# Side matrix products between attention steps: from pairs of groups that end together to a staggered chain, with one product of each step moved forward

## The chip, the cores and the metric

The kernel runs on one core of one Trainium2 chip. The metric is the device time of one execution in microseconds; the kernel before takes 1770.66 us in the median of three runs (1768.67 to 1771.16). TensorE does matrix products into PSUM (8 banks of 128 partitions x 512 float32), VectorE, ScalarE and GpSimd do elementwise work and reductions, SyncE issues the transfers. In the profile they are PE (its weight loads PEld), DVE, ACT, POOL and SP.

## The reference, cut to what matters

One transformer block on a sequence of 2048 rows of 512 numbers: a layer norm with a scale and shift that come from a condition vector, attention with 32 query heads of 16 numbers over one shared key and value head, a gated addition, a second such norm, and a bilinear gated feed-forward layer of width 1792.

```python
sa, ca, ga, sb, cb, gb = mod(silu(c) @ w_mod)          # six rows of 512
h = layernorm(x) * (1 + ca) + sa
q = (h @ wq) as 32 heads of 16;  k = h @ wk;  v = h @ wv
p = softmax(q k^T * 16**-0.5)
x = x + ga * ((p v) @ wo)
h = layernorm(x) * (1 + cb) + sb
x = x + gb * (((h @ w_gate) * (h @ w_up)) @ w_down)
```

## The kernel before

**Attention.** The 2048 queries are cut into four blocks of 512 (NB). A block has eight units of four heads, so there are 32 units, and a unit has 32 steps: 16 tiles of 128 keys, each taken by two steps (a = 0 and a = 1). The 1024 steps form the main loop (line 1162). One step issues on PE, in this order:

- one maxima product, `mx` (`max_mm`, line 556): raw scores of a later unit, 128 queries x 512 keys. DVE reduces them to row maxima (line 566, `mpart<-mx`). There are two PSUM banks for `mx` (NMX = 2). The maxima become an extra row of the query operand later, so that the exponential needs no further shift. They run 38 iterations (LEAD) ahead of the scores.
- the first piece of P times V, `pv` (line 604): float32, 4 x 256 columns, for a tile of an earlier step. It is run by the hardware as two passes.
- one scores product, `sc` (`qk_exp`, line 596), which ACT turns into exponentials P (line 602). It has two PSUM banks (NSC = 2), and a third one, `spare`, only while side products don't hold that.
- the second piece of P times V,
- the second maxima product and the second scores product.

All these use half of PE's rows. `mx` and `sc` of a step use row half a; `pv` uses the other half, so that the two streams can run at the same time. Each product is issued as four matmuls of 32 output partitions (`quarters`, line 474).

**Side products.** Whatever else needs PE is fitted in at the end of steps: the projections to queries (`q_proj`, 12 products of 128 rows deep per group), the output projection (`wo_work`, 12 per group), and the feed-forward layer (`ffn_work`: 14 gate groups and 14 up groups of 12, then 4 down groups of 42). A product that is 128 rows deep is split into two row halves, one for each half of PE; both halves of a product, or of two different groups, issued one behind the other, are called a pair here. Row halves may not write to the same PSUM bank at the same time. So `duo` (line 485) takes two groups with two banks, `misc` and `spare`: in its first turn group 0 uses the upper rows and group 1 the lower rows, in its second turn they change places. After the second turn both groups are complete, and both are evicted: the first at once, the second in the middle of the next step (`drain_mids`, line 1184). Evictions of gate and up groups are ACT copies (lines 789 and 796); those of the output projection and the down groups are DVE operations (lines 703 and 814).

**Pacing.** `pace` spreads the queued pairs over the steps up to their due step; `fill_gap` (line 1077) issues up to 3 pairs (BURST) at the end of a step out of a credit. Between the two turns of a duo there lies one step, with a semaphore through a one-element GpSimd memset (`token`, line 499), or two steps (SWAP_WAIT) while the early weight work is still queued; behind a duo the next one may start two steps later (GROUP_WAIT). What is not placed in the loop, above all the feed-forward layer of the last block, runs after it as whole 128x128 products (`plain`, line 518).

Of the kernel before, what the change touches and what calls it, by code (L numbers as in the profile page):

```python
# [13 lines left out]
F32 = mybir.dt.float32  # L14
# [6 lines left out]
KC = D // 128  # L21
# [3 lines left out]
NU = NB * UB  # L25
# [29 lines left out]
def adaln_mqa_glu_kernel(ctx: ExitStack, tc: tile.TileContext, x_in, wq_in, wk_in, wv_in, wo_in,  # L55
# [412 lines left out]
    class Group:  # L468


        def __init__(self, n, op, pre, post, mid=True):
            self.n, self.op, self.pre, self.post, self.mid = n, op, pre, post, mid

    def quarters(p, left, right, start=True, stop=True):
        return [nc.tensor.matmul(p[c:c + CW, :], left[:, c:c + CW], right, start=start, stop=stop)  # L475
# [6 lines left out]
    token = consts.tile([1, 1], F32, name="token")  # L482
    SYNC = mybir.DependencyInfo(mybir.DependencyClass.Sync, mybir.DependencyReason.DATA)

    def duo(g0, g1, tags=("misc", "spare")):

        ps = g0.pre(tag=tags[0]), g1.pre(tag=tags[1])
        n = g0.n
        mark = None
        for turn in range(2):  # L490
            for i in range(n):
                for r in range(2):
                    ms = half(ps[r ^ turn], (g0, g1)[r ^ turn], i, r, turn == 0 and i == 0,
                              turn == 1 and i == n - 1)
                    if mark is not None:
                        tc.add_manual_dep(ms[0].ins, mark.ins.name, SYNC, reason="row halves of one bank in turn")
                        mark = None
                if turn == 0 and i == n - 1 and cur["mark"]:
                    mark = nc.gpsimd.memset(token, 0.0)  # L499
                    tc.add_manual_dep(mark.ins, ms[-1].ins.name, SYNC, reason="end of a row half")  # L500
                if turn == 0 or i < n - 1:
                    yield i == n - 1
        g0.post(ps[0])

        def late():
            g1.post(ps[1])
            after(3, free)

        def free():
            spare["held"] -= 1  # L510

        spare["held"] += 1
        if g1.mid:
            mids.append(late)
        else:
            after(2, late)

    def plain(g):
        p = g.pre()
# [7 lines left out]
    def q_proj(b, ch):  # L527

        def evac(p):
            q16 = work.tile([128, 2, BT], F16, name="q16", tag="ev", bufs=3)  # L530
            qf = work.tile([128, BT], F32, name="qf", tag="ev", bufs=3)
            nc.scalar.activation(qf, p, AF.Copy, scale=qvs[:, 0:1])  # L532
# [11 lines left out]
        return Group(3 * KC, op, ps_misc, evac, mid=False)  # L544

    def load_q(u):
        b, g = divmod(u, UB)
# [502 lines left out]

    side = deque(wlist)
    fill = deque()
    cur = {"gen": None, "left": 0, "swapped": -9, "wait": 0, "mark": False}
    credit = [0.0]

    def pace(step):

        n, most = cur["left"], 0.0
        if n:
            most = n / max((cur["due"] - step) / 2, 1.0)  # L1060
        for _, kind, what, due in fill:
            n += 4.0 if kind == "solo" else 2 * what[0].n
            kept = RESERVE / PAIR if due > (NB * UB - 1) * NSTEP else 0.0
            most = max(most, (n - kept) / max((due - step) / 2, 1.0))
        return most

    def open_gate(step):
        if not fill or (fill[0][1] == "duo" and step < cur["wait"]):
            return False
        if fill[0][1] == "duo" and NU * NSTEP - step < 2 * -(-fill[0][2][0].n // BURST) + 2:  # L1070
            return False
        gate = fill[0][0]
        if gate[0] is None:
            gate[0] = step + gate[1]
        return gate[0] <= step

    def fill_gap(step):


        if cur["gen"] is None:  # L1080
            if not open_gate(step):
                return
            _, kind, what, due = fill.popleft()
            if kind == "solo":
                _, f, post = what
                credit[0] -= 4.0
                f()
                if post:
                    posts.append(post)
                return  # L1090
            begin(step, what, due)
        if cur["second"] and step < cur["swapped"] + (1 if cur["mark"] else SWAP_WAIT):
            return
        n = min(int(credit[0]), BURST)
        if not cur["second"]:
            n = max(n, -(-cur["turn"] // max(NU * NSTEP - 6 - step, 1)))
        burst(step, max(1, min(n, cur["turn"])))

    def begin(step, two, due, tags=("misc", "spare")):
        cur.update(gen=duo(*two, tags=tags), left=2 * two[0].n, turn=two[0].n, second=False, due=due, swapped=-9,  # L1100
                   mark=not side)

    def burst(step, n):
        for _ in range(n):
            swap = next(cur["gen"], None)
            credit[0] -= 1.0
            cur["left"] -= 1
            cur["turn"] -= 1
            if swap is None:
                cur["gen"], cur["left"], cur["wait"] = None, 0, step + GROUP_WAIT  # L1110
                return
            if swap:
                cur["turn"], cur["second"], cur["swapped"] = cur["left"], True, step
                return

    side_next = [0.0]

    def side_step(step):
        if side and step >= side_next[0] and (step % 2 or side[0][1] is nothing):
# [31 lines left out]
            posts.append(v_out)  # L1151
    assert cur["gen"] is None
    for two in qtwos:
        fill.append(([0, 0], "duo", two, QDUE))
    credit[0] = 0.0

    def ffn_twos(b):
        gu, down = ffn_work(b)
        return gu + twos(down)

    early["on"] = False
    for u in range(NU):
# [3 lines left out]
        for i in range(NSTEP):  # L1166
            step = u * NSTEP + i
            kt, p = divmod(i, 2)
            drain_posts()
            spare["scores"] = not spare["held"] and cur["gen"] is None and not (fill and fill[0][1] == "duo" and open_gate(step))  # L1170
# [18 lines left out]
            if fill or cur["gen"]:  # L1189
                credit[0] = min(credit[0] + pace(step) / 2, 6.0)  # L1190
                if credit[0] >= 1.0:
                    fill_gap(step)
            side_step(step)
            if u > 0 and g % 2 == 0 and i in (5, 9, 15):
                if i == 5:
                    nrm = normalise((u - 1) // UB, ((u - 1) % UB) // 2)
                nrm[(5, 9, 15).index(i)]()
            if i == 16 and u > 0 and g == 0:
                ln = ln2_work(b - 1)
                due = (b + 1) * UB * NSTEP + (DUE if b < NB - 1 else LAST_DUE)  # L1200
                gate = [step + 4, 0]
                for two in twos(wo_work(b - 1)):
                    fill.append((gate, "duo", two, due))
# [3 lines left out]
                for two in ffn_twos(b - 1):  # L1207
                    fill.append((gate, "duo", two, due))

    def drain_all():  # L1210
        for t in sorted(timers):
# [9 lines left out]
    pv_lower(u)  # L1221
    pv(u, KT - 1, 1)
    pv_out(u)
    left = cur["left"]
    if cur["gen"] is not None:
        assert cur["second"] and NU * NSTEP - cur["swapped"] > 2
        for _ in cur["gen"]:
            drain_posts()
        drain_mids()
    ring["tags"] = [("misc", 1), ("spare", 1)] + [("mx", NMX)] * NMX + [("sc", NSC)] * NSC  # L1230
    tail = deque(plain(g) for _, _, two, _ in fill for g in two)

# [10 lines left out]
            for _ in plain(g):  # L1243
                pass

    cover(6000 - 216 * left)
    nrm = normalise(NB - 1, KC - 1)
    nrm[0]()
    cover(3000)
# [31 lines left out]
```

## Time and profile before

| | |
|---|---|
| median of three runs | 1770.66 us |
| the profiled execution, its own time | 1768.31 us |
| its span, first to last instruction | 1766.5 us |
| mean granted TensorE clock | 0.995 |
| before the main loop's first scores product | about 92 us |
| main loop | about 92 to 1600 us |
| behind the loop | about 1600 to 1766 us |

The span is cut by the table of stages: the units of the query projections (92 to 447 us), then for each block three units' worth of time with the output projection and the norm (447 to 544, 840 to 939, 1233 to 1330) and the long runs of the feed-forward products (544 to 840, 939 to 1233, 1330 to 1563). PE is called busy from a matmul's start to its modelled end; matmuls on the two row halves overlap, so that a PE that is busy all the time can still have one of its halves idle. The starts in the timeline tell more than the busy share.

### The profile page before, as it was taken

How to read it: one execution, taken by the hardware profiler on the slowest of the kernel's cores; microseconds unless marked ns; L12 is line 12 of the kernel's file. 1: busy time of each engine (PE TensorE's matmuls, PEld its weight loads, DVE VectorE, ACT ScalarE, POOL GpSimd, SP SyncE). 2: the span in 40 equal slices, each digit the busy share in tenths (PEclk: the TensorE clock that was granted, in tenths of full speed). 3: DMA queues.
4: the chain of work that ended last, by engine and by line, in shares of the span. 5: the costliest groups of instructions: out<-in, count | busy, mean ns of one | idle time of the engine just before them, and what ended most of it. 6: DMA issues, size and time to landing. Idle time of an engine off the chain costs nothing. (4 is left out here: it accounts for less than half of the span.)

```text
span 1766.5 us, 102784 instructions
## 1 busy us (share of the span) xinstructions
PE 1697.3 (96%) x47395; PEld 1062.5 (60%) x47395; DVE 1438.7 (81%) x2353; ACT 1258.7 (71%) x2319; POOL 562.8 (32%) x788
## 2 busy tenths in 40 slices
PE   6899999999999999999999999999999999999999
PEld 3345555555556666776656766677656666754444
DVE  7899999999998888888999888899999998922210
ACT  3478888878877777777777777777788887883110
POOL 5714454537567852210032222100032121221130
PEclk9999999999999999999999999999999999999999
DMA  5212222212222210000100000000100000001000
GB/s 195 101 31 81 61 81 63 83 42 84 77 75 68 62 27 20 6 18 24 43 23 19 13 18 14 8 18 23 49 17 19 12 19 12 14 7 41 19 0 24
DMA packets 49179, 71.09 MB, mean 40 GB/s; under 512 B 15270, under 2 KB 29418, under 8 KB 48748
## 3 DMA queue, kind: packets, MB, share of 16 engines
q1 hardware_dynamic: 47164, 64.33, 12.2%
q8 instruction: 370, 6.06, 1.5%
q14 instruction: 61, 0.50, 0.1%
q10 hardware_dynamic: 1584, 0.20, 0.1%
HBM read 51.12 MB, written 8.92 MB: 34 GB/s over the span
## 5 line engine op out<-in xcount | busy, mean ns | idle before, releaser
L566 DVE TENSOR_REDUCE mpart<-mx 128x1 f32<-128x512 f32 x2048 | 1325.0, 686 | 123.8 <-PE mx L475 46.4
L602 ACT ACTIVATE P<-sc 128x512 f32<-128x512 f32 x2048 | 1133.9, 599 | 301.0 <-PE sc L475 194.0
L614 PE MATMUL pv<-P,vst 64*32 64x256 f32 x16384 | 1089.4, 379 | 0.8 <-ACT ev L622 0.7
L475 PE MATMUL mx<-kst,sst 48*32 48x512 f16 x8192 | 815.9, 383 | 36.1 <-DVE mpart L566 28.1
L475 PE MATMUL sc<-sst,kst 50*32 50x512 f16 x8192 | 824.9, 379 | 8.4 <-ACT P L602 6.8
L614 PEld LDWEIGHTS pv<-P,vst 64*32 64x32 f32 x16384 | 486.1, 106 | 93.5 <-issue 3.2
L475 PEld LDWEIGHTS <-sst 48*32 48x32 f16 x8192 | 340.0, 90 | 295.5 <-issue 222.1
L475 PEld LDWEIGHTS <-kst 50*32 50x32 f16 x8192 | 284.1, 91 | 78.5 <-issue 50.5
L475 PE MATMUL misc<-h2T,wg 64*32 64x512 f16 x4032 | 297.5, 376 | 1.1 <-issue 1.1
L475 PE MATMUL misc<-h2T,wu 64*32 64x512 f16 x4032 | 297.6, 376 | 0.0
L797 POOL TENSOR_TENSOR gf<-gf,g 128x512 f32<-128x512 f32 x42 | 53.6, 1276 | 346.5 <-ACT gf L796 346.5
L475 PEld LDWEIGHTS <-wu 64*32 64x32 f16 x4032 | 115.8, 92 | 30.2 <-issue 1.6
L475 PEld LDWEIGHTS <-wg 64*32 64x32 f16 x4032 | 115.3, 92 | 19.1 <-issue 2.6
L475 PE MATMUL misc<-wd,glu 64*32 64x512 f16 x2688 | 121.6, 376 | 0.0
L475 PE MATMUL misc<-h,wq 64*32 64x512 f16 x1536 | 100.6, 377 | 2.1 <-ACT qf L532 2.1
L499 POOL MEMSET token<- 1x1 f32 x43 | 3.8, 88 | 283.8 <-PE misc L475 242.4
L789 ACT ACTIVATE g<-misc 128x512 f32<-128x512 f32 x56 | 33.6, 600 | 76.6 <-PE misc L522 75.5
L522 PE MATMUL misc<-wd,glu 128*128 128x512 f16 x336 | 73.2, 379 | 0.0
L475 PEld LDWEIGHTS <-glu 64*32 64x32 f16 x2688 | 60.0, 92 | 17.7 <-issue 1.3
L801 POOL TENSOR_TENSOR glu<-gf,glu 128x512 f16<-128x512 f32 x56 | 65.1, 1163 | 4.7
L799 DVE TENSOR_TENSOR gf<-misc,g 128x512 f32<-128x512 f32 x14 | 9.7, 692 | 62.9 <-PE misc L522 62.9
L627 DVE SCALAR_TENSOR_TENSOR ev<-pv,evs,ev 128x512 f32<-128x512 f32 x32 | 23.8, 743 | 44.7 <-ACT ev L622 44.7
(232 smaller groups left out, 1062.6 us busy)
## 6 DMA issues: line engine op xcount, KB each, us to landing
wsl<-in_B_w_gate_dram SPq DMA_DIRECT2D x32, 224.0 KB
wsl<-in_B_w_up_dram SPq DMA_DIRECT2D x32, 224.0 KB
wsl<-in_B_w_down_dram SPq DMA_DIRECT2D x28, 256.0 KB
sst<-qd SPq DMA_DIRECT2D x186, 32.0 KB
qd<-q SPq DMA_DIRECT2D x16, 256.0 KB
oc<-ev SPq DMA_DIRECT2D x128, 32.0 KB
rr<-ri SPq DMA_DIRECT2D x16, 256.0 KB
xl<-in_A_x_dram SPq DMA_DIRECT2D x16, 256.0 KB
```

Source lines behind the costliest of these rows:

```text
L475: return [nc.tensor.matmul(p[c:c + CW, :], left[:, c:c + CW], right, start=start, stop=stop) for c in range(0, 128, CW)]
L499: mark = nc.gpsimd.memset(token, 0.0)
L522: nc.tensor.matmul(p, left, right, start=i == 0, stop=i == g.n - 1)
L566: nc.vector.tensor_reduce(mparts[u][:, a, p, t, kc:kc + 1], m, axis=AX.X, op=OP.max)
L602: nc.scalar.activation(ptl[u, kt, a][:, p, :], t, AF.Exp)
L614: nc.tensor.matmul(pvb[u, r][32 * j:32 * j + 32, c * w:(c + 1) * w], vst[ks, kt, :], ptl[u, kt, a][ks, p, c * w:(c + 1) * w], start=(kt == ...
L627: nc.vector.scalar_tensor_tensor(ev, pvb[u, 1], evs, ev, op0=OP.mult, op1=OP.add)
L789: nc.scalar.activation(st["g", f], p, AF.Copy, scale=2.0 ** -45)
L797: nc.gpsimd.tensor_tensor(gf, gf, st["g", f], op=OP.mult)
L799: nc.vector.tensor_tensor(gf, p, st["g", f], op=OP.mult)
L801: nc.gpsimd.tensor_tensor(st["glu"][:, 1, f, :], gf, st["glu"][:, 0, f, :], op=OP.subtract)
```

## The change

`duo` stays for the lead alone. In the main loop the side products become a chain of turns. A turn has two segments, one for each row half: a new group's upper rows on one bank, and the lower rows of the group before it (the carried one) on the other. At a turn's end the carried group is complete and is evicted at once, and the new one becomes the carried one; the next group takes the bank just evicted. A turn with an eviction at its end is followed by a wait to the next step (EV_WAIT = 1), any other by two steps (SWAP_WAIT). A chain's first and last turn have one segment only. The two 42-deep down groups are taken as a pair with turns of 12, 30 and 42 products and a last one of 12. The token and its memset are gone. In the step, the second maxima product goes in front of the second piece of P times V.

```diff
-GROUP_WAIT = 2
+EV_WAIT = 1
+TURN = 12
+    class Run:
+        def __init__(self, g, tag):
+            self.g, self.tag, self.p, self.k, self.u = g, tag, None, 0, 0
+        def emit(self, i, r):
+            if self.p is None:
+                self.p = self.g.pre(tag=self.tag)
+            half(self.p, self.g, i, r, self.k == 0, self.k == 2 * self.g.n - 1)
+            self.k += 1
...
-                if turn == 0 and i == n - 1 and cur["mark"]:
-                    mark = nc.gpsimd.memset(token, 0.0)
-                    tc.add_manual_dep(mark.ins, ms[-1].ins.name, SYNC, reason="end of a row half")
...
+    def plan(step):
+        if cur["stages"]:
+            segs, wait = cur["stages"].popleft()
+            begin_turn(segs, cur["end"] + wait)
+            return True
+        carry = cur["carry"]
+        seg_u = (carry, carry.u, carry.g.n) if carry else None
+        if fill and fill[0][1] == "prod" and open_gate(step):
+            _, _, gs, due = fill.popleft()
+            cur["due"] = due
+            tag = other(carry.tag) if carry else "misc"
+            if not carry:
+                spare["held"] += 1
+            if len(gs) == 1:
+                x = Run(gs[0], tag)
+                begin_turn(((x, 0, x.g.n), seg_u), cur.get("end", -9) + (EV_WAIT if cur["evicted"] else SWAP_WAIT))
+                cur["carry"] = x
+                return True
...
+        if carry:
+            begin_turn((None, seg_u), cur["end"] + SWAP_WAIT)
+            cur["carry"] = None
+            return True
...
+    def burst_turn(step, n):
+        for _ in range(n):
+            j = cur["j"]
+            more = False
+            for r, seg in enumerate(cur["segs"]):
+                if seg and seg[1] + j < seg[2]:
+                    seg[0].emit(seg[1] + j, r)
+                    credit[0] -= 0.5
+                    more = more or seg[1] + j + 1 < seg[2]
+            cur["j"] += 1
+            if not more:
+                end_turn(step)
+                return
+
+    def end_turn(step):
+        done = {id(seg[0]): seg[0] for seg in cur["segs"] if seg and seg[0].k == 2 * seg[0].g.n}
+        for x in done.values():
+            x.g.post(x.p)
+        cur.update(segs=None, end=step, evicted=bool(done))
...
             max_half(a, 0, 2)
             pv(*who, 0)
             qk_exp(u, kt, 0, a)
+            max_half(a, 1, 2)
             pv(*who, 1)
             drain_mids()
-            max_half(a, 1, 2)
             qk_exp(u, kt, 1, a)
```

Three places show what moves. First, PE's order inside one step of the main loop, where the first scores product ends (`kst` and `sst` are the key and query operands, `sst_120` those of a later unit). Before:

```order
L475 LDWEIGHTS kst
L475 MATMUL sc<-sst_119,kst 32x512
L614 MATMUL pv<-P,vst 32x256 x4
L475 LDWEIGHTS sst_120
L475 MATMUL mx<-kst,sst_120 32x512
```

and now, from the second maxima product on:

```order
L487 LDWEIGHTS sst_120
L487 MATMUL mx<-kst,sst_120 32x512
L612 MATMUL pv<-P,vst 32x256 x4
L487 LDWEIGHTS kst
L487 MATMUL sc<-sst_119,kst 32x512
```

The second piece of P times V (`pv`) stood ahead of the second maxima product and stands behind it now.

Second, ACT's order in the units with gate and up groups (`g` and `gf` are the two evictions, `P` the exponentials, two in a step). Before:

```order
L789 ACTIVATE g<-misc 128x512
L602 ACTIVATE P<-sc 128x512
L796 ACTIVATE gf<-misc 128x512
L602 ACTIVATE P<-sc 128x512 x19
L789 ACTIVATE g<-misc 128x512
```

and now:

```order
L794 ACTIVATE gf<-misc 128x512
L600 ACTIVATE P<-sc 128x512 x10
L787 ACTIVATE g<-misc 128x512
L600 ACTIVATE P<-sc 128x512 x10
L794 ACTIVATE gf<-misc 128x512
```

Two evictions with one exponential between them every ten steps have become one eviction every five steps.

Third, DVE's order at the end of two down groups (`x` is the eviction, `mpart` the maxima). Before:

```order
L566 TENSOR_REDUCE mpart<-mx 128x1 x12
L814 SCALAR_TENSOR_TENSOR x_13083<-misc,sca,x_13083 128x512
L566 TENSOR_REDUCE mpart<-mx 128x1
L814 SCALAR_TENSOR_TENSOR x_13109<-misc,sca,x_13109 128x512
L566 TENSOR_REDUCE mpart<-mx 128x1 x33
```

and now:

```order
L564 TENSOR_REDUCE mpart<-mx 128x1 x8
L812 SCALAR_TENSOR_TENSOR x_13034<-misc,sca,x_13034 128x512
L564 TENSOR_REDUCE mpart<-mx 128x1 x10
L812 SCALAR_TENSOR_TENSOR x_13326<-misc,sca,x_13326 128x512
L564 TENSOR_REDUCE mpart<-mx 128x1 x28
```

The two evictions are ten reductions, five steps, apart instead of one reduction.

More of the change, by code (lines that the diff above doesn't have):

```diff
@@ L492, in duo @@
                 for r in range(2):
[L493 to L497, printed above, removed]
-                if turn == 0 and i == n - 1 and cur["mark"]:
-                    mark = nc.gpsimd.memset(token, 0.0)
-                    tc.add_manual_dep(mark.ins, ms[-1].ins.name, SYNC, reason="end of a row half")
+                    half(ps[r ^ turn], (g0, g1)[r ^ turn], i, r, turn == 0 and i == 0, turn == 1 and i == n - 1)
                 if turn == 0 or i < n - 1:
@@ L512, in duo @@
         spare["held"] += 1
[L513 to L516, printed above, removed]
+        after(2, late)
     def plain(g):
@@ L1061, in pace @@
         for _, kind, what, due in fill:
-            n += 4.0 if kind == "solo" else 2 * what[0].n
+            n += 4.0 if kind == "solo" else sum(g.n for g in what)
             kept = RESERVE / PAIR if due > (NB * UB - 1) * NSTEP else 0.0
@@ L1067, in open_gate @@
     def open_gate(step):
-        if not fill or (fill[0][1] == "duo" and step < cur["wait"]):
+        if not fill:
             return False
-        if fill[0][1] == "duo" and NU * NSTEP - step < 2 * -(-fill[0][2][0].n // BURST) + 2:
+        if fill[0][1] == "prod" and NU * NSTEP - step < 2 * sum(g.n for g in fill[0][2]) / 2.5 + 4:
             return False
@@ L1075, in open_gate, with other @@
         return gate[0] <= step
-    def fill_gap(step):
[L1080 to L1092, printed above, removed]
+    def other(tag):
+        return "spare" if tag == "misc" else "misc"
@@ L1093, in fill_gap @@
+    def fill_gap(step):
+        if cur["segs"] is None and not plan(step):
+            return
+        if step < cur["wait"]:
             return
         n = min(int(credit[0]), BURST)
-        if not cur["second"]:
-            n = max(n, -(-cur["turn"] // max(NU * NSTEP - 6 - step, 1)))
-        burst(step, max(1, min(n, cur["turn"])))
+        late = -(-seg_left() // max(NU * NSTEP - 8 - step, 1))
+        burst_turn(step, max(1, n, int(late)))
+    def burst_turn(step, n):
[10 more added lines that the diff above has]
+                end_turn(step)
+                return
@@ L1099, in begin, with free_spare @@
+    def end_turn(step):
[3 more added lines that the diff above has]
+        cur.update(segs=None, end=step, evicted=bool(done))
+        if not cur["stages"] and not cur["carry"]:
+            after(4, free_spare)
+    def free_spare():
+        spare["held"] -= 1
+    side_next = [0.0]
     def begin(step, two, due, tags=("misc", "spare")):
-        cur.update(gen=duo(*two, tags=tags), left=2 * two[0].n, turn=two[0].n, second=False, due=due, swapped=-9,
-                   mark=not side)
+        cur.update(gen=duo(*two, tags=tags), due=due)
@@ L1103, in burst @@
     def burst(step, n):
         for _ in range(n):
[L1105 to L1110, printed above, removed]
+            if next(cur["gen"], None) is None:
+                cur["gen"] = None
                 return
-            if swap:
-                cur["turn"], cur["second"], cur["swapped"] = cur["left"], True, step
-                return
@@ L1153, in adaln_mqa_glu_kernel @@
     for two in qtwos:
-        fill.append(([0, 0], "duo", two, QDUE))
+        for g in two:
+            fill.append(([0, 0], "prod", (g,), QDUE))
     credit[0] = 0.0
+    cur.update(end=-2, evicted=False)
     def ffn_twos(b):
         gu, down = ffn_work(b)
-        return gu + twos(down)
+        return [(g,) for two in gu for g in two] + twos(down)
     early["on"] = False
@@ L1169, in adaln_mqa_glu_kernel @@
             drain_posts()
-            spare["scores"] = not spare["held"] and cur["gen"] is None and not (fill and fill[0][1] == "duo" and open_gate(step))
+            spare["scores"] = not spare["held"] and not (fill and fill[0][1] == "prod" and open_gate(step))
             a = p
@@ L1201, in adaln_mqa_glu_kernel @@
                 gate = [step + 4, 0]
-                for two in twos(wo_work(b - 1)):
-                    fill.append((gate, "duo", two, due))
+                for gr in wo_work(b - 1):
+                    fill.append((gate, "prod", (gr,), due))
                 for gap, it in zip((TR_GAP, 0, 0, 0), ln):
@@ L1206, in adaln_mqa_glu_kernel @@
                 gate = [None, 0]
-                for two in ffn_twos(b - 1):
-                    fill.append((gate, "duo", two, due))
+                for gs in ffn_twos(b - 1):
+                    fill.append((gate, "prod", gs, due))
     def drain_all():
@@ L1223, in adaln_mqa_glu_kernel @@
     pv_out(u)
[L1224 to L1229, printed above, removed]
+    assert not live()
+    drain_mids()
     ring["tags"] = [("misc", 1), ("spare", 1)] + [("mx", NMX)] * NMX + [("sc", NSC)] * NSC
```

47 lines of the change are left out of this document (36 added, 11 removed).

## The prediction

> **What bounds the kernel now.** I read the page's busy shares first, then the table of busy time by stage, then the timeline of single steps.
>
> ```profile
> PE 1697.3 (96%) x47395; PEld 1062.5 (60%) x47395; DVE 1438.7 (81%) x2353; ACT 1258.7 (71%) x2319; POOL 562.8 (32%) x788
> ...
> 92.00:447.00 355.00, 342.16 (x9623) 192.29 (x9627) 338.00 (x565) 297.19 (x540) 160.88 (x174) 1.00 0.22 65
> ...
> 544.00:840.00 296.00, 289.34 (x9762) 201.90 (x9754) 259.67 (x408) 226.48 (x425) 103.88 (x114) 1.00 0.11 29
> ...
> 1600.00:1766.50 166.50, 161.01 (x816) 73.80 (x805) 29.24 (x47) 17.55 (x28) 32.54 (x60) 1.00 0.07 22
> ```
>
> The columns behind the times are the busy time of PE, PEld, DVE, ACT and POOL. PE looks full in every stage, but a step can be long while one of PE's halves is idle, and the share doesn't say so. In the loop DVE is also busy 88 to 95% (259.67 of 296.00, 338.00 of 355.00). The last 166 us hold almost nothing but whole products, 732 of them in both programs; they don't change. Everything therefore hangs on how long one of the 1024 steps takes, and that shows in a stretch in which each step carries two pairs:
>
> ```profile
> 1432.56 3.45 DVE L566 TENSOR_REDUCE mpart<-mx 128x1 f32<-128x512 f32 x5
> 1432.71 0.40 PE L475 MATMUL mx<-kst,sst 48*32 48x512 f16 x4
> 1432.74 0.40 PE L614 MATMUL pv<-P,vst 64*32 64x256 f32 x4
> 1432.93 0.40 PE L475 MATMUL sc<-sst,kst 50*32 50x512 f16 x4
> 1432.96 0.61 PE L614 MATMUL pv<-P,vst 64*32 64x256 f32 x8
> 1433.30 0.40 PE L475 MATMUL mx<-kst,sst 48*32 48x512 f16 x4
> 1433.51 1.09 ACT L602 ACTIVATE P<-sc 128x512 f32<-128x512 f32 x2 [0.24 <-PE sc L475]
> 1433.60 0.40 PE L475 MATMUL misc<-h2T,wg 64*32 64x512 f16 x4
> 1433.73 0.40 PE L475 MATMUL misc<-h2T,wu 64*32 64x512 f16 x4
> 1434.04 0.40 PE L475 MATMUL mx<-kst,sst 48*32 48x512 f16 x4
> 1434.17 0.40 PE L614 MATMUL pv<-P,vst 64*32 64x256 f32 x4
> 1434.63 0.40 PE L475 MATMUL mx<-kst,sst 48*32 48x512 f16 x4
> 1434.94 1.09 ACT L602 ACTIVATE P<-sc 128x512 f32<-128x512 f32 x2 [0.34 <-PE sc L475]
> 1435.46 0.40 PE L475 MATMUL mx<-kst,sst 48*32 48x512 f16 x4
> ```
>
> A product holds its half for 0.22 us (1432.71 to 1432.93), a pass of P times V as well (1432.74 to 1432.96). So a step needs 4 x 0.22 = 0.87 us of each half, and each pair 0.22 more. The second maxima product could start at 1433.15, 0.22 behind the scores product, but starts at 1433.30: it waits for DVE to free one of its two banks. By then the second piece of P times V, at 1433.17 (the second pass in the row of 1432.96), is under way on the other half. Two steps take 1435.46 - 1432.71 = 2.75 us, 1.375 each, where the halves need 0.87 + 2 x 0.22 = 1.31. A step with three pairs needs 0.87 + 0.65 = 1.52 and is bound by PE; one with no or one pair is bound by the two banks and DVE:
>
> ```profile
> 237.64 3.85 DVE L566 TENSOR_REDUCE mpart<-mx 128x1 f32<-128x512 f32 x6
> ```
>
> Six reductions, the last 0.69 long, start every (3.85 - 0.69)/5 = 0.632 us: 1.26 us for a step's two. This is the floor of any step with maxima.
>
> **The change part by part.** *The pairs.* Counted in the two orders, the loop holds 1656 pairs in both. Before, 304 steps have three, 269 two, 451 one or none. Now 250 have three, 301 two, 428 one or none, and 45 have three halves on one side only, which hold that half for 0.65 us like three pairs. At 1.52, 1.375 and 1.26 us that is 462 + 370 + 568 = 1400 before and (295 steps at 1.52) 448 + 414 + 539 = 1401 now. The staggering as such gives +1 us; the chain's single halves eat what the evener steps save. Its own error is small: 0.01 us on the 428 light steps would be 4 us, and nearly as much before.
>
> *Two evictions at once become two apart.* This is the gain. The end of a pair of gate and up groups before:
>
> ```profile
> 750.31 0.40 PE L475 MATMUL mx<-kst,sst 48*32 48x512 f16 x4
> ...
> 751.51 0.40 PE L475 MATMUL mx<-kst,sst 48*32 48x512 f16 x4
> ...
> 752.33 0.40 PE L475 MATMUL mx<-kst,sst 48*32 48x512 f16 x4
> 752.88 0.40 PE L475 MATMUL sc<-sst,kst 50*32 50x512 f16 x4 [0.16 <-ACT P L602]
> ...
> 753.57 0.39 PE L475 MATMUL mx<-kst,sst 48*32 48x512 f16 x4
> ```
>
> ```profile
> 750.76 0.60 ACT L789 ACTIVATE g<-misc 128x512 f32<-128x512 f32 x1
> 751.26 0.60 ACT L602 ACTIVATE P<-sc 128x512 f32<-128x512 f32 x1
> 751.73 0.61 ACT L796 ACTIVATE gf<-misc 128x512 f32<-128x512 f32 x1
> 752.21 1.71 ACT L602 ACTIVATE P<-sc 128x512 f32<-128x512 f32 x3
> ```
>
> ACT is fully occupied from 750.76 on, each eviction takes about 0.49 us of its time (751.26 to 751.73 for an exponential, 751.73 to 752.21 for an eviction), and PE's scores product at 752.88 stands waiting for a bank. The step without pairs and the one behind it with three take 753.57 - 750.31 = 3.26 us, against 1.26 + 1.52 = 2.78. The double eviction costs 0.48 us, and there are 42 (the up group's evictions in the loop):
>
> ```profile
> L796 ACT ACTIVATE gf<-misc 128x512 f32<-128x512 f32 x42 | 25.7, 613 | 0.0
> ```
>
> 42 x 0.48 = 20 us. Of these 20 the chain gives back what two single evictions cost. In the stretch with two pairs ACT idles 0.24 and 0.34 us per step, so one eviction makes it 0.15 to 0.25 late, once; and the bank that the exponential of 1433.51 leaves at 1434.11 isn't written again before 1434.26 (0.22 behind 1434.04), 0.15 of slack. That leaves 0 to 0.10 us: I take 0.05, 84 x 0.05 = 4 us. The ends: nothing at all (0), or what an eviction costs where steps have no slack, in the query projections:
>
> ```profile
> 247.11 1.08 ACT L602 ACTIVATE P<-sc 128x512 f32<-128x512 f32 x2
> 248.06 0.71 ACT L532 ACTIVATE qf<-misc,qvs 128x512 f32<-128x512 f32 x1
> 248.63 1.11 ACT L602 ACTIVATE P<-sc 128x512 f32<-128x512 f32 x2
> ```
>
> There a step with one takes 1.52 (247.11 to 248.63), 0.26 over the floor: 84 x 0.26 = 22 us, which would undo it all. I stay near the low end because the chain's steps are those of the first stretch. Query evictions cost the same in both kernels: they already lie in steps of their own (+0).
>
> *DVE's evictions* of the 12 output-projection and 12 down groups:
>
> ```profile
> 804.68 0.74 DVE L814 SCALAR_TENSOR_TENSOR x<-misc,sca,x 128x512 f32<-128x512 f32 x1
> 805.34 0.68 DVE L566 TENSOR_REDUCE mpart<-mx 128x1 f32<-128x512 f32 x1
> 805.94 0.74 DVE L814 SCALAR_TENSOR_TENSOR x<-misc,sca,x 128x512 f32<-128x512 f32 x1
> ```
>
> Each adds 0.66 us to DVE (804.68 to 805.34). Apart, steps with three pairs (1.52 against DVE's 1.26) can hide 0.26 of it: 24 x 0.26 = -6 us at best. Against it, the next group now wants the evicted bank one step later, where the old duo left two steps; where the eviction ends behind that step's second scores product, PE stands still with all that is queued behind it (the next step's maxima and scores), at most the 0.26 that the eviction sticks out: +6. I take 0.
>
> *The token* was a GpSimd memset off the path, hidden behind a whole step; its removal is worth 0.
>
> *The second maxima product in front of the second piece of P times V.* A matmul that waits for a semaphore holds everything behind it in PE's order. Before, that was the scores product, on the same half anyhow. Now P times V, on the other half, is held too. Worked through for the stretch above: P times V starts at 1433.30 in place of 1433.17, its half is free after 0.43 + 2 x 0.22 at 1434.17, not 1434.04, so the next step begins 0.13 later; but its second maxima product started at 1434.63 because of DVE and still does (1434.17 + 0.43 = 1434.60). Both halves are then free at 1434.63 + 0.43 + 0.43 = 1435.49 instead of 1435.46. The two steps lose 0.03 us, 0.017 each: 301 x 0.017 = 5 us. With three pairs the wait is mostly gone before the product's turn; for these 295 I take a third of it, 2 us; steps with fewer have room. Sum +7. Upper end: nothing of the 0.13 is made up and one of the halves in two steps pays it, 551 steps x 0.065 = +36. Below nothing: the product could start 0.02 earlier (1433.15 against 1433.17) in those 551 steps, if P times V held it back today: -11. This row speaks against that:
>
> ```profile
> 753.96 0.40 PE L614 MATMUL pv<-P,vst 64*32 64x256 f32 x4
> 754.01 0.39 PE L475 MATMUL mx<-kst,sst 48*32 48x512 f16 x4
> 754.18 0.40 PE L614 MATMUL pv<-P,vst 64*32 64x256 f32 x4
> ```
>
> The second maxima product starts at 754.01, ahead of the second piece at 754.18, though that stands in front of it: when nothing waits for a semaphore, one half overtakes the other. The Trainium skill states the opposite ("TensorE: Matmul & The Clock Gate", Part 3, "The mechanism"): matmuls start and end strictly in program order, only weight loads are pulled ahead. By that rule this edit would give the 11 us; the trace, with a start 0.17 us ahead of the order, disagrees.
>
> *Sum:* +1 - 20 + 4 + 0 + 7 = -8 us. The profiled execution took 1768.31 us, so it would take 1760; it stands 2.35 us below the median of the runs, so the median would be 1770.66 - 8 = 1763 us.
>
> **The rivals.** *Slower, by held P times V.* The place is the second maxima product of steps with two or three pairs. For it: it starts late in the stretch above, and DVE is the fuller the evener the pairs lie. Against it: the next step's wait takes most of the delay back. The other terms give -15; it decides from 15/551 = 0.027 us per step on. At the full 0.065 the sum is -15 + 36 = +21, 1792 us; at two thirds of that, +9, 1780 us.
>
> *No change: an eviction costs the same wherever it lies.* Then 42 x 0.48 comes back as 84 x 0.24, near the row of the query projections, and with the order free the sum is +1: 1772 us. For it: ACT's work is the same. Against it: ACT idles in the steps where the single ones will stand.
>
> *A larger gain:* single evictions vanish in ACT's idle time, DVE's are hidden by steps with three pairs and the new order gives rather than takes: +1 - 20 - 6 = -25 with the order at 0, 1746 us, or 1735 with its -11.
>
> **How the numbers follow.** Forecast (1755 to 1767) 0.43, the larger gain 0.15 (0.03 of it with the -11), no change 0.20, slower 0.22. This kernel's measurement can't tell less than 0.2%, 3.5 us, from no change: faster means below 1767, slower above 1774. So the forecast and the larger gain make 0.58 faster; 1772 is the 0.20 of no change; 1780 and 1792 are the 0.22. The predicted time is 1763 us. The range goes from the larger gain's 1746 to just over the slower case's milder form, 1782, which leaves out the -11 and the full 0.065; the forecast's own is 1755 to 1770.
>
> **What would show it.** In the changed kernel's timeline: ACT evictions one at a time with no scores product waiting for ACT behind them (step two right if that idle is gone); the distance from one gate eviction to the next but one shorter than now, where 13 of them give (750.8 - 559.8)/12 = 15.9 us:
>
> ```profile
> L789 ACT ACTIVATE g<-misc x13: 597/597/606, 559.8 to 750.8; 128x512 f32<-128x512 f32 x13
> ```
>
> The order's cost shows where a step has two pairs: if the second piece of P times V starts with the second maxima product, and a step takes 1.39 us, that step is right; 1.44 and more would be the rival. The forecast is wrong if steps with single evictions take over 0.2 us more than their neighbours, or if PE stands waiting for DVE's evictions at the first product of a new output-projection or down group.

## The result and the profile after

The changed kernel takes 1739.57 us (median of 4 runs, 1738.83 to 1740.90) against 1769.66 us before (4 runs, 1766.76 to 1771.16): a ratio of 0.9832, interval 0.9817 to 0.9846, so 30 us less. A later set of runs gave 0.9825 (0.9810 to 0.9839). The forecast was 1763 us, and the time lies below the whole range of 1746 to 1782. The direction was right; the size was not, by 23 us.

The page of the changed kernel opens like this (columns as before: busy time, share of the span, instructions; then the largest group of DVE with its busy time, mean ns of one, and the idle time before it):

```profile
span 1739.1 us, 102797 instructions
...
PE 1686.9 (97%) x47395; PEld 972.1 (56%) x47395; DVE 1406.3 (81%) x2353; ACT 1253.0 (72%) x2319; POOL 560.1 (32%) x745
...
L564 DVE TENSOR_REDUCE mpart<-mx 128x1 f32<-128x512 f32 x2048 | 1290.8, 683 | 125.1 <-PE mx L487 110.5
```

The same group on the page of the kernel before:

```profile
L566 DVE TENSOR_REDUCE mpart<-mx 128x1 f32<-128x512 f32 x2048 | 1325.0, 686 | 123.8 <-PE mx L475 46.4
```

The shares tell nothing again: PE is at 97% instead of 96%. But the 2048 reductions, the same work, cover 1290.8 us instead of 1325.0, with nearly the same mean duration (683 and 686 ns). More of them overlap their neighbours. That is the first trace of the cause.

By stage, the table of busy time of the changed kernel (start and end, length, then PE, PEld, DVE, ACT, POOL), cut at the same units of the loop as the three rows in the prediction:

```profile
92.00:433.40 341.40, 333.78 (x9635) 177.55 (x9639) 330.75 (x567) 297.77 (x541) 161.06 (x174) 1.00 0.23 67
...
533.90:825.70 291.80, 289.91 (x9901) 186.07 (x9897) 253.48 (x408) 225.11 (x425) 99.23 (x100) 1.00 0.11 30
...
1572.80:1739.10 166.30, 160.62 (x808) 73.58 (x802) 29.23 (x47) 17.16 (x27) 32.65 (x60) 0.99 0.07 22
```

The last stage is unchanged, as forecast (166.30 and 166.50 us). The stage full of gate and up groups, where the prediction had put its gain, is only 4.2 us shorter (296.00 to 291.80). The first stage, the units with few pairs, where it had put nothing, is 13.6 us shorter (355.00 to 341.40).

What the prediction wanted looked at shows as follows. First, ACT's timeline in a step with a single eviction (start, duration, what ended the idle time before it):

```profile
562.88 1.08 ACT L600 ACTIVATE P<-sc 128x512 f32<-128x512 f32 x2 [0.49 <-PE sc L487]
563.85 0.60 ACT L794 ACTIVATE gf<-misc 128x512 f32<-128x512 f32 x1
564.33 1.10 ACT L600 ACTIVATE P<-sc 128x512 f32<-128x512 f32 x2
565.95 1.09 ACT L600 ACTIVATE P<-sc 128x512 f32<-128x512 f32 x2 [0.51 <-PE sc L487]
```

and PE's around it:

```profile
564.06 0.40 PE L487 MATMUL sc<-sst,kst 50*32 50x512 f16 x4
...
565.15 0.40 PE L487 MATMUL mx<-kst,sst 48*32 48x512 f16 x4
565.18 0.39 PE L612 MATMUL pv<-P,vst 64*32 64x256 f32 x4
565.37 0.40 PE L487 MATMUL sc<-sst,kst 50*32 50x512 f16 x3
```

The eviction takes its 0.48 us (563.85 to 564.33) out of an idle time that its neighbours show as 0.49 and 0.51, and the next scores product starts 0.22 behind its maxima product (565.15 to 565.37): nothing waits for ACT. Over the whole program PE's waits (us in total, times, longest) were before

```profile
PE mx L475 <- DVE mpart L566: 28.1, 75, 1.2
PE sc L475 <- ACT P L602: 6.8, 27, 0.3
```

and are now

```profile
PE mx L487 <- DVE mpart L564: 19.2, 45, 1.3
PE sc L487 <- ACT P L600: 2.0, 2, 1.8
```

The 27 waits for ACT have become two. Behind the waits shown, the list names no wait of PE for DVE's evictions of output-projection or down groups. The distance of one gate eviction from the next but one, 15.9 us before, is now (736.7 - 540.2)/13 = 15.1 us, from the row of these evictions in the window 530 to 830 us:

```profile
L787 ACT ACTIVATE g<-misc x14: 597/603/604, 540.2 to 736.7; 128x512 f32<-128x512 f32 x14
```

Second, PE's timeline in a stretch in which each step carries two pairs:

```profile
1371.58 0.40 PE L487 MATMUL mx<-kst,sst 48*32 48x512 f16 x4
...
1372.09 0.40 PE L487 MATMUL mx<-kst,sst 48*32 48x512 f16 x4
1372.10 0.42 PE L612 MATMUL pv<-P,vst 64*32 64x256 f32 x4
...
1372.99 0.40 PE L487 MATMUL mx<-kst,sst 48*32 48x512 f16 x4
...
1374.35 0.40 PE L487 MATMUL mx<-kst,sst 48*32 48x512 f16 x4
```

The second piece of P times V now starts with the second maxima product (1372.10 and 1372.09), and two steps take 1374.35 - 1371.58 = 2.77 us, 1.385 each. The prediction had given 1.39. Here its picture holds; over all steps with two pairs the median is 1.371 us (1.406 before). It fails in steps with less on PE. DVE's timeline at the place that answers to the six reductions of before:

```profile
230.68 3.08 DVE L564 TENSOR_REDUCE mpart<-mx 128x1 f32<-128x512 f32 x5
```

Five reductions, the last 0.68 long, start every (3.08 - 0.68)/4 = 0.600 us; before it was 0.632. A step's two reductions take 1.20 us, and the 1.26 that the prediction called the floor of any step with maxima was none.

### The profile page after: what moved, and what is told of

Read it like the earlier page. It is cut to its first block, busy times and chain, and to the rows that moved or that the text cites. A ratio compares the mean times of both kernels' runs of the same rounds, so it can differ in the third digit from the quotient of the medians.

```text
span 1739.1 us, 102797 instructions
## 1 busy us (share of the span) xinstructions
PE 1686.9 (97%) x47395; PEld 972.1 (56%) x47395; DVE 1406.3 (81%) x2353; ACT 1253.0 (72%) x2319; POOL 560.1 (32%) x745
## 5 line engine op out<-in xcount | busy, mean ns | idle before, releaser
L564 DVE TENSOR_REDUCE mpart<-mx 128x1 f32<-128x512 f32 x2048 | 1290.8, 683 | 125.1 <-PE mx L487 110.5
L612 PE MATMUL pv<-P,vst 64*32 64x256 f32 x16384 | 1172.3, 383 | 0.3 <-issue 0.3
L487 PE MATMUL mx<-kst,sst 48*32 48x512 f16 x8192 | 819.8, 382 | 25.9 <-DVE mpart L564 19.2
L612 PEld LDWEIGHTS pv<-P,vst 64*32 64x32 f32 x16384 | 418.2, 105 | 56.5 <-issue 5.3
L487 PEld LDWEIGHTS <-kst 50*32 50x32 f16 x8192 | 303.3, 91 | 75.7 <-issue 32.8
L487 PE MATMUL misc<-h2T,wg 64*32 64x512 f16 x4032 | 307.1, 379 | 0.3
L487 PE MATMUL misc<-h2T,wu 64*32 64x512 f16 x4032 | 305.1, 376 | 0.7 <-issue 0.2
L487 PE MATMUL misc<-wd,glu 64*32 64x512 f16 x2688 | 114.1, 376 | 0.1
L652 POOL TENSOR_TENSOR oc<-oc,rr 128x512 f32<-128x512 f32 x15 | 19.3, 1285 | 213.7 <-DMA rr<-ri 186.2
L487 PE MATMUL misc<-h,wq 64*32 64x512 f16 x1536 | 85.0, 378 | 0.6
L487 PEld LDWEIGHTS <-glu 64*32 64x32 f16 x2688 | 53.1, 93 | 26.1 <-issue 6.0
L625 DVE SCALAR_TENSOR_TENSOR ev<-pv,evs,ev 128x512 f32<-128x512 f32 x32 | 23.8, 743 | 45.1 <-ACT ev L620 36.4
```

What stands on the lines that cost most here:

```text
L564: nc.vector.tensor_reduce(mparts[u][:, a, p, t, kc:kc + 1], m, axis=AX.X, op=OP.max)
L612: nc.tensor.matmul(pvb[u, r][32 * j:32 * j + 32, c * w:(c + 1) * w], vst[ks, kt, :], ptl[u, kt, a][ks, p, c * w:(c + 1) * w], start=(kt == ...
L625: nc.vector.scalar_tensor_tensor(ev, pvb[u, 1], evs, ev, op0=OP.mult, op1=OP.add)
L652: eng.tensor_tensor(o, o, st["r"], op=OP.mult)
```

## The experiments

Two theories were set against each other after the result. The **holding theory** is the prediction's: what is new in PE's order only decides which matmul has to stand behind one that waits for a semaphore. The **signal theory**: what counts is when the end of a product is told to the engine that waits for it. A product on one half may start ahead of matmuls that stand in front of it in the program, but its signal comes only when all matmuls in front of it have ended too. Then the old order held back the signal of each second maxima product until the second piece of P times V in front of it was through, and the reduction, not the product, was late.

### The order alone and the chain alone

The order alone, in the kernel before:

```diff
             qk_exp(u, kt, 0, a)
+            max_half(a, 1, 2)
             pv(*who, 1)
             drain_mids()
-            max_half(a, 1, 2)
             qk_exp(u, kt, 1, a)
```

> The kernel before with one edit: the second maxima product in front of the second piece of P times V; the side products stay in pairs of groups. Signal theory (new): the signal that a product is done isn't given before every matmul that stands ahead of it in PE's order has ended. Before, the second maxima product's signal therefore waits for the second piece of P times V (0.14 us behind the product's end at 239.40 us, against 0.02 for the first maxima product), and every second reduction starts late; with the edit that is gone. Expected: 15 to 22 us less than before (about 13 of them in the first nine units, whose steps go from 1.28 to about 1.23 us), near 1750 us. The prediction's theory: the order costs 7 us, 1777 us.

The chain alone: the changed kernel with that edit taken back.

```diff
             qk_exp(u, kt, 0, a)
-            max_half(a, 1, 2)
             pv(*who, 1)
             drain_mids()
+            max_half(a, 1, 2)
             qk_exp(u, kt, 1, a)
```

> The changed kernel with the old order inside the step: the chain alone. Signal theory: what is left for the chain, 8 to 14 us less than before, 1756 to 1762 us, with the steps of the first units back at 1.28 us. The prediction's theory: 15 us less than before, 1755 us. If both parts were only worth something together, this one and the order alone would add up to clearly less than 30 us.

Measured: the order alone 1746.99 us, ratio 0.9891 (0.9875 to 0.9908); the chain alone 1757.09 us, ratio 0.9940 (0.9919 to 0.9960). 1.09% and 0.60% make 1.69%, and the whole change gave 1.68%: within the intervals, some 5 us, the two parts add up without helping or hurting each other. Two thirds of the gain, 19 us, come from the edit that the prediction had priced at +7.

The steps of the loop can be grouped by the pairs that they hold, since the order alone leaves the pairs where they were. From the start of each step's first scores product to that of the next, summed from the two traces:

| pairs in the step | steps | order alone against before, us |
|---|---|---|
| none | 243 | -8.6 |
| one | 206 | -8.9 |
| two | 269 | -1.4 |
| three | 304 | -0.3 |
| all | 1022 | -19.2 |

17.5 of the 19.2 us lie in steps with at most one pair. There the median step without pairs, in the seven units with query projections, went from 1.281 to 1.229 us.

The chain alone leaves PE three waits of scores products for ACT, in place of 27:

```profile
PE sc L487 <- ACT P L600: 2.2, 3, 1.8
```

So the evictions' mechanism works without the order, too.

### What the trace shows of the signal

In the kernel before, PE's timeline of a step without pairs:

```profile
238.63 0.62 PE L614 MATMUL pv<-P,vst 64*32 64x256 f32 x8
239.00 0.40 PE L475 MATMUL mx<-kst,sst 48*32 48x512 f16 x4
239.06 0.40 PE L614 MATMUL pv<-P,vst 64*32 64x256 f32 x4
```

and DVE's reductions there:

```profile
238.87 0.68 DVE L566 TENSOR_REDUCE mpart<-mx 128x1 f32<-128x512 f32 x1
...
239.56 0.69 DVE L566 TENSOR_REDUCE mpart<-mx 128x1 f32<-128x512 f32 x1
```

The product of 239.00 is the second maxima product. It starts ahead of the last pass of the second piece of P times V (239.06), which stands in front of it in the program. Its end is 239.40; the pass ends at 239.46. The semaphore that DVE waits for rises at 239.54 by the trace's semaphore events, 0.14 behind the product's end and 0.07 behind the pass's, and the reduction starts at 239.56, 0.69 behind the one before it. In the changed kernel, where P times V stands behind the product:

```profile
232.62 0.40 PE L487 MATMUL mx<-kst,sst 48*32 48x512 f16 x4
232.63 0.62 PE L612 MATMUL pv<-P,vst 64*32 64x256 f32 x6
```

```profile
232.49 1.28 DVE L564 TENSOR_REDUCE mpart<-mx 128x1 f32<-128x512 f32 x2
```

The second of these two reductions starts 1.28 - 0.68 = 0.60 behind the first, at 233.09, and 0.07 behind the product's end of 233.02. It overlaps the end of the first. For all products of the loop the traces give these median distances from the (modelled) end of a product to the rise of PE's semaphore that belongs to it, in ns (the rises are counted off in the order of the program):

| kernel | first maxima | second maxima | first scores | second scores |
|---|---|---|---|---|
| before | 24 | 164 | 113 | 25 |
| order alone | 24 | 24 | 94 | 112 |
| chain alone | 24 | 165 | 108 | 25 |
| changed | 24 | 24 | 84 | 112 |
| P times V first | 229 | 24 | 44 | 112 |
| scores ahead | 24 | 24 | 24 | 24 |

The last two kernels are the next experiments. Late are the products that have a piece of P times V directly in front of them in the order, if that piece is not yet through when they are. In the kernel before, that is so for the second maxima product in 74% of the steps, and there the semaphore follows the end of the piece, not of the product, at a nearly constant distance: 74 ns in the median, 61 to 87 in nine steps of ten. The others follow their own end by 24 to 46 ns in the median. With the scores ahead there is a piece in front of the second maxima product as well, but it has started earlier and is mostly over.

DVE goes by that semaphore. When it rises in time, a reduction starts 0.60 to 0.61 us behind the one before it; when it rises later, the reduction starts 0.023 us behind the rise (medians of the loop, in the kernel before and in the changed one). So each hundredth of a us by which the signal is too late is a hundredth more between two reductions.

### The first piece of P times V ahead of the first maxima product

If the signal theory holds, the old penalty can be had again, at the other product.

```diff
-            max_half(a, 0, 2)
             pv(*who, 0)
+            max_half(a, 0, 2)
             qk_exp(u, kt, 0, a)
```

> The changed kernel with the first piece of P times V in front of the first maxima product (nothing else moves). Both start at the same time on their two halves, and the piece's second pass ends about 0.23 us behind the maxima product. Signal theory: the first maxima product's signal comes about 0.28 us later, so the floor of a step goes from 1.20 to about 1.45 us: 80 to 130 us more than the changed kernel, 1820 to 1870 us. If what counts is only when a product may start, nothing starts later here: within 5 us of the changed kernel.

Measured: 1801.93 us, ratio 1.0201 (1.0181 to 1.0222), 62 us slower than the changed kernel by the medians and 65 by the ratios. PE's timeline in it

```profile
230.99 0.40 PE L487 MATMUL mx<-kst,sst 48*32 48x512 f16 x4
231.18 0.40 PE L612 MATMUL pv<-P,vst 64*32 64x256 f32 x4
```

and DVE's:

```profile
231.67 3.78 DVE L564 TENSOR_REDUCE mpart<-mx 128x1 f32<-128x512 f32 x6 [0.22 <-PE sc L487]
```

The maxima product ends at 231.39; DVE idles 0.22 us and starts only at 231.67, 0.09 behind the end of P times V's second pass (231.58). (The view names the scores product as what ended the idle time; both products raise the same semaphore.) The holding theory had allowed no more than a few us; it can't explain this. The signal theory had the sign and the place, but not the size: 62 to 65 where 80 to 130 was expected. Of the 59.6 us between the two traces 8.6 lie in steps without pairs, 21.4 in those with one, 23.8 in those with two and 6.9 in those with three. Part of the delay is thus taken up by slack that the expectation didn't count; how much by which slack was not separated.

### Both scores products ahead of P times V

If signals were all that counts, ACT's should come at once too:

```diff
             max_half(a, 0, 2)
-            pv(*who, 0)
             qk_exp(u, kt, 0, a)
+            pv(*who, 0)
             max_half(a, 1, 2)
+            qk_exp(u, kt, 1, a)
             pv(*who, 1)
             drain_mids()
-            qk_exp(u, kt, 1, a)
```

> The changed kernel with each scores product in front of the piece of P times V that it follows now (maxima, scores, piece, maxima, scores, piece). Signal theory: in the changed kernel the scores products' signals still come 0.11 and 0.07 to 0.10 us behind their ends because of the pieces ahead of them; here 0.02, and ACT starts that much earlier. DVE sets the light steps, so only steps that wait for ACT gain: 3 to 10 us less than the changed kernel, 1730 to 1737 us. The prediction's theory: a scores product that waits for ACT now holds P times V as well: 0 to 7 us more than the changed kernel.

Measured: 1745.74 us, ratio 0.9883 (0.9867 to 0.9900), that is 6 us slower than the changed kernel by the medians and 9 by the ratios, with an interval that doesn't touch its. All signals now come 24 ns behind their products in the median (table above), and it is no gain. PE's timeline shows what else moved:

```profile
233.77 0.40 PE L487 MATMUL mx<-kst,sst 48*32 48x512 f16 x4
233.90 0.42 PE L612 MATMUL pv<-P,vst 64*32 64x256 f32 x4
```

The second piece of P times V starts 0.13 behind the second maxima product, where in the changed kernel it starts 0.01 behind it. Over the loop the median is 0.013 us in the changed kernel, and here 0.037 in steps without pairs and 0.084 with one. The delay begins at the first piece. In steps with one pair, in the units with query projections, this piece starts 0.14 us behind the first maxima product instead of 0.01; all that follows on its half is late with it, and the next step's first product, on the same half, starts at 1.35 instead of 1.28 (medians). In these units the median step without pairs gained (1.229 to 1.182 us) and that with one pair lost (1.271 to 1.359). Between the two traces all steps without pairs are 3.5 us shorter, those with one 6.1 and those with three 4.8 us longer. So P times V can be held by what stands in front of it, as the prediction said, and here that costs more than the earlier signals give. That the early signals to ACT bring nothing against it fits ACT's idle time of 0.5 us a step, shown above.

A milder form, only the first scores product ahead of the first piece:

```diff
-            pv(*who, 0)
             qk_exp(u, kt, 0, a)
+            pv(*who, 0)
             max_half(a, 1, 2)
```

> The changed kernel with only the first scores product in front of the first piece of P times V. Signal theory: its signal comes 0.02 instead of 0.09 to 0.11 us behind its end; alone that would give up to 3 us. Holding theory (from the run with both scores products ahead, which was 6 us slower than the changed kernel): a piece of P times V that is issued 0.22 us later leaves its half idle, and the half is late at the step's end; the first piece is later by 0.22 us, the second one follows it directly, by about 0.05 us: 0 to 4 us more than the changed kernel. With both: 1737 to 1743 us.

Measured: 1745.29 us, from two runs that lie far apart (1741.25 and 1749.33), ratio 0.9851 (0.9811 to 0.9891). One of the two lies in the expected 1737 to 1743. That can't be told from the changed kernel's 0.9832 and settles nothing.

### The evictions made small

To measure the evictions' cost by itself, they were cut from 512 to 64 columns, in the kernel before:

```diff
-                nc.scalar.activation(st["g", f], p, AF.Copy, scale=2.0 ** -45)
+                if b < NB - 1:
+                    nc.scalar.activation(st["g", f][:, 0:64], p[:, 0:64], AF.Copy, scale=2.0 ** -45)
...
-                    nc.scalar.activation(gf, p, AF.Copy)
-                    nc.gpsimd.tensor_tensor(gf, gf, st["g", f], op=OP.mult)
+                    gs = work.tile([128, 64], F32, name="gs", bufs=2)
+                    nc.scalar.activation(gs, p[:, 0:64], AF.Copy)
```

followed by the same product on GpSimd, over 8 copies of the 64 columns; and the same in the changed kernel.

> The kernel before with the evictions of the gate and up groups in the loop cut to 64 of 512 columns on ACT (GpSimd then multiplies those 64 columns eight times over; the feed-forward layer of the first three blocks comes out wrong). It prices the double evictions. The prediction's price: 42 x 0.48 = 20 us for two whole ones; with about a third of ACT's time left in them, 12 to 18 us less than before, 1749 to 1755 us. If the double eviction costs little, and the long step behind it is the pairs' own time: under 6 us.

> The changed kernel with the same cut of the 84 evictions (same part of the result wrong). It prices single evictions. The prediction's price, 0.05 us each with 4 us in all: 2 to 4 us less than the changed kernel, 1736 to 1738 us. If a single eviction costs what it does in the query projections, 0.26 us: 14 us or more less, under 1726 us.

Measured: in the kernel before 1756.01 us, ratio 0.9901 (0.9869 to 0.9932), a gain of 17.5 us (12 to 23; 15 by the medians); in the changed kernel 1735.94 us, ratio 0.9806 (0.9779 to 0.9833), some 5 us less than its 0.9832, with overlapping intervals. ACT's timeline of the first shows what is left of an eviction, at the place where the prediction read the double one:

```profile
750.06 0.60 ACT L602 ACTIVATE P<-sc 128x512 f32<-128x512 f32 x1 [0.22 <-PE sc L475]
750.55 0.22 ACT L800 ACTIVATE gs<-misc 128x64 f32<-128x64 f32 x1
750.65 1.78 ACT L602 ACTIVATE P<-sc 128x512 f32<-128x512 f32 x3
```

0.10 us of ACT's time (750.55 to 750.65) instead of 0.48. What the chain could win on evictions is the difference of the two gains, 17.5 - 4.6 = 13 us, give or take 8 by their intervals, and with the evictions cut in both kernels the change is still worth 0.9901 - 0.9806, 0.95% or 17 us: about the order's 19. The profiled execution of the first, the slowest of its four, shows the gain where the double evictions lay (-4.1 us in steps without pairs, -8.0 in those with three), but 6.2 us more in steps with two, so that only 5.1 of it remained in the loop. So the cost of a double eviction is 17.5/42 = 0.42 us, from 0.29 to 0.55 by the interval; 0.48 lies inside.

### A mixed order, and the changed kernel once more

The scores ahead of P times V only where a step holds no pairs, since there it gained (184 of the 1024 steps); where it has some, the order of the changed kernel:

```diff
+            if filled(step):
...
+            else:
+                qk_exp(u, kt, 0, a)
+                pv(*who, 0)
+                max_half(a, 1, 2)
+                qk_exp(u, kt, 1, a)
+                pv(*who, 1)
+                drain_mids()
```

> The changed kernel with both scores products ahead of the pieces only in steps that carry no side products (184 of 1024). There the half that holds P times V has time to spare and the signals count: steps of 1.19 in place of 1.23 us, as in the run with the order everywhere. Signal and holding theory together: 3 to 8 us less than the changed kernel, 1732 to 1737 us. If that run's short steps were short at their neighbours' cost: no change or slower.

Measured: 1739.75 us, ratio 0.9824 (0.9798 to 0.9850). To tell it from the changed kernel, both ran again beside each other:

> The changed kernel itself, on one chip with the next one, so that the two can be told apart by less than 0.3%. Expected again 0.982 to 0.985 of the kernel before.

> The version with the scores products ahead of the pieces in steps without side products, beside the changed kernel. If the short steps are worth their own gain (0.04 us in some 155 of them): 3 to 8 us less than the changed kernel. If their neighbours give it back: within 2 us of it.

Measured: the changed kernel 1737.57 us, ratio 0.9825 (0.9810 to 0.9839); the mixed order 1735.79 us, 0.9810 (0.9796 to 0.9825). The difference of 1.8 us is not shown: the intervals overlap. At 184 steps x 0.047 us (1.229 to 1.182, the medians above) 8 to 9 us were to be had; in the trace of the mixed order the steps without pairs were shorter by 2.4 in all. Why not more is open.

## Why the prediction was wrong

**The second maxima product in front of the second piece of P times V** is the step that failed: +7 us in the sum, -19 measured. By itself that is a miss of 26 us; the other terms, -15 in the sum and -10 measured, took a little of it back, and 23 remained. Two sentences of it are to be kept apart. For steps with two and three pairs it gave +5 and +2; measured were -1.4 and -0.3, so little was amiss there, and the step of 1.385 us is the 1.39 that it named. But "steps with fewer have room" priced the other 450 at nothing, and there lay 17.5 us. The reason stands in the floor that the prediction took from six reductions, 1.26 us for a step's two. It read the spacing of 0.632 us as DVE's own speed. In the units with query projections the spacings were by turns 0.69 us, where the signal had been held back by P times V, and 0.61 (medians); in the changed kernel they are 0.60 and 0.61. A floor read from a stretch in which the engine looked busy was the very delay that the edit removes.

P times V is held, as the prediction said: over the loop the second piece starts 0.013 us behind the second maxima product (median), and where that product had waited for DVE, the piece's half had been idle for some 0.1 us in steps with at most one pair and at most 0.05 with more. What this costs by itself was not separated from what the earlier signal gives.

The prediction had asked about the overtaking, but only of starts: that the second maxima product starts at 754.01, ahead of P times V at 754.18, it took as proof that nothing is held back. What follows on a product waits for its signal, not for its start. At that very place the signal is late. The product ends at 754.40; P times V's second pass follows on the other half, and DVE's reductions are these:

```profile
754.39 0.40 PE L614 MATMUL pv<-P,vst 64*32 64x256 f32 x4
```

```profile
754.04 0.69 DVE L566 TENSOR_REDUCE mpart<-mx 128x1 f32<-128x512 f32 x1 [0.57 <-PE mx L475]
754.89 2.10 DVE L566 TENSOR_REDUCE mpart<-mx 128x1 f32<-128x512 f32 x3 [0.15 <-PE sc L475]
```

The pass ends at 754.79, the semaphore rises at 754.87, 0.47 behind the product's end, and DVE, idle for 0.15 us, starts at 754.89. By the Trainium skill ("TensorE: Matmul & The Clock Gate", Part 3, "The mechanism") matmuls start and end strictly in program order, so that one semaphore on the last of them is enough. For starts, and for ends as the profile models them, this case's traces say otherwise (starts at 239.00 ahead of 239.06, ends at 239.40 ahead of 239.46); for the signals they agree (164 ns behind the product's end with P times V in front, 24 without). The prediction dismissed the rule with the half of it that the trace refutes, and gave the rival that went with it, 1735 us, a chance of 0.03. The measured 1739.57 is 4.6 us from that, though by other sizes of the terms.

**Two evictions at once become two apart**, -20 + 4, was right in its mechanism: single evictions disappear in ACT's idle time (563.85), the waits for ACT went from 27 to 2. In its size it was somewhat high. The chain alone gave -10 us (-7 to -14) where -15 stood for the pairs, the double and the single evictions together; cutting the evictions says 13 where 16 stood, too near to tell apart. The 0.48 us was the excess of two steps over 1.26 + 1.52, and both of these are bounds that steps seldom reach: with the evictions cut, the median step without pairs took 1.33 us and the one with three 1.56 in the stage full of gate and up groups (544 to 840 us). Over these, the 3.26 us of the two steps leave 0.37. The 0.05 for a single one fits the 4.6/84 = 0.05 that the changed kernel shows, though that isn't resolved.

**The pairs**, +1, and **the token**, 0: nothing speaks against them, and neither was run alone. **DVE's evictions**, 0: no wait of PE for them appeared. The steps with three halves on one side, which the prediction counted like three pairs, differ from one execution of the same kernel to the next by 3.9 us, all 45 together, so a few us there mean nothing.

**The rivals.** "Slower, by held P times V" is real as a mechanism (0.013 us, above, and the kernel with both scores products ahead), but the steps that it named, with two or three pairs, did not get longer. "An eviction costs the same wherever it lies" is out: cutting it is worth 17.5 us where it is double and some 5 where it is single. "A larger gain" had the sign of the order right, in its form with -11, and its evictions wrong.

## What to carry to other kernels

Where the engine that limits a step waits for a short matmul, put it in front of long independent matmuls in PE's order, even if these run on the other half and don't delay its start. For ACT, which had time to spare, the same move gained nothing here. Before calling a spacing of an engine's instructions its floor, compare the end of each producer with the start of its consumer: a steady gap of more than the usual one (here 0.16 against 0.07 us) is a signal that comes late. An eviction is cheapest alone, in the idle time of a step.

## What the runs showed of the hardware

PE's two halves start matmuls out of program order, but the signal of a matmul waits for everything in front of it: for a maxima product it came 24 ns behind its own end with nothing unfinished in front, and 164 and 229 ns (medians) with two passes of P times V in front, 74 ns behind the end of the last of them. And DVE's reductions of 128x512 from PSUM follow each other every 0.60 us when the signal is there in time, the next starting before the last has ended; when it comes late, they start 0.023 us behind it.
